# Regrouping the weight conversion and moving state products in the first sixteen tiles of a fused attention and cosine-gated MLP

## The chip, the cores and the metric

One core of a Trainium2 chip. The metric is the device time of one launch in microseconds (us). The kernel before took 815.66 us (median of 6 runs; 815.76 in the 3 runs that the prediction had). Comparisons are made against runs of the kernel before on the same chip in the same rounds; three chips were used for the experiments, so times are compared through their ratio to before.

## The reference, cut to what matters

```python
def _attn_ref(x, state):                      # x (8,8,512,64), state (8,8,32,64)
    scores = scale * x @ state^T;  a  = softmax(scores);  xread = a @ state
    scores2 = scale * state @ x^T; a2 = softmax(scores2); sread = a2 @ x
    return concatenate([xread, sread], axis=2)
def _moe_ref(x, w_in, w_out):                 # x (8*544, 512), weights (512,2048), (2048,512)
    h = x @ w_in
    g = h * cos(h)
    return g @ w_out
```
The weights arrive as float64 and are turned into float32 on the chip.

## The kernel before

Batch b has 16 tiles of 128 hidden columns each. A tile's h comes from the read weights aT and from state products `sw` (state times w_in, one product for four tiles); then g = h·cos h, then output matmuls some tiles later. In batch 0 fourteen of the sixteen steps also convert one 128x1024 load of weights, in six parts on three engines:

```python
        if p == "1":    # ScalarE: high words, absolute value
            nc.scalar.activation(dst, raw.bitcast(F32)[:, :, :, 1], func=ACTF.Abs)
        elif p == "2":  # ScalarE: low words
            nc.scalar.activation(e, raw.bitcast(U32)[:, :, :, 0], func=ACTF.Copy, ...)
        elif p == "a":  # VectorE: limit (L225)
            engine = nc.gpsimd if i == 1 else nc.vector
            engine.tensor_scalar(dst, dst, 2.0 ** -15, None, op0=ALU.max)
        elif p == "b":  # VectorE: shift (L227)
            nc.vector.tensor_scalar(bits, bits, 3, None, op0=ALU.logical_shift_left)
        elif p == "c":  # VectorE: sign (L230)
            nc.vector.scalar_tensor_tensor(out=bits, in0=raw[:, :, :, 1], scalar=-2 ** 31, ...)
        else:           # "d", GpSimd: addition (L240)
            n = 1 if i < 4 else 2
            for j in range(n):
                ...
                nc.gpsimd.tensor_tensor(bits[:, r], bits[:, r], e.bitcast(I32)[:, r], op=ALU.add)
...
    def gate(t):   ... # ScalarE: q = h + MAGIC           (L449)
    def gate2(t):  ... # VectorE: subtract, S below       (L452)
    def gate3(t):  ... # ScalarE: Abs, then Sin           (L457, L458)
    def gate4(t):  ... # VectorE: g = h * q, M below      (L464)
...
    for step, t in enumerate(tiles()):
        ...
        hidden(t)                       # TensorE: h
        go(0)                           # attention work on TensorE
        gate(t); gate2(t); go(1); go(3)
        if last >= 0: convert(last, "cd")
        if conv >= 0 and not todo[1]: convert(conv, "1")
        gate3(t)
        gate4(t)
        ...
        if conv >= 0: convert(conv, "2")
        go(4)
        if conv >= 0: convert(conv, "ab")
        ...
        while len(line) >= (LAG if step >= NH else LAG + 1):   # LAG = 3, NH = 8
            output(line.pop(0))
```
The program puts the h accumulator in PSUM and gives it two buffers. The lag is the number of tiles by which the output matmuls stay behind. The order of the work on each engine is written by hand (no scheduler).

"Cold" and "warm" below mean TensorE at a low and at full granted clock: in the kernel before the four matmuls of h(16) took 3.51 us (granted clock 0.57 from 119 to 123 us), those of h(17) 1.88 us (1.00 from 123 to 127 us); from 22.1 to 25.0 us, under the first two h, the clock was 0.50. "The lock" is a name for a wait that the traces show: a limit or shift that meets a GpSimd instruction of the addition ends only after that instruction. In the kernel before the shift at 55.83 took 1.65 us and ended 0.56 us after the addition; at 31.55, with GpSimd idle, it took 0.69 us. S and M, which have h in PSUM as an operand, show no such wait: beside an addition M at 54.06 took 0.69 us in the kernel before, and S at 59.84 took 0.69 us in the changed kernel.

## Time and profile before

| | before |
|---|---|
| median | 815.66 us |
| TensorE busy, of the 813.0 us span | 778.6 us (96%) |
| VectorE, ScalarE, GpSimd busy | 434.5, 398.3, 183.4 us |
| first state products, start | 20.56 us |
| h of tile 16, of tile 17, start | 119.36, 125.75 us |

The whole-span shares say only that TensorE is the resource in the long run. What can be won is in the first 125 us, and it is read from that stretch: which wait ends last before each h. The prediction shows those lines.

### The profile page before, as it was taken

The numbers are of one execution on the slowest core, as the hardware profiler recorded it, in microseconds if no ns is written. First come the engines' busy times: TensorE is split into PE (matmuls) and PEld (weight loads), VectorE is DVE, ScalarE is ACT, GpSimd is POOL, SyncE is SP. The second block draws the span as 40 slices with busy tenths as digits, with TensorE's granted clock in tenths as the row PEclk, the third lists the DMA queues.
The fourth block names the chain that finished last, engine by engine and source line by source line (L and its number), as shares of the span: only waits on it lengthen the run. The fifth ranks groups of instructions, "written<-read, shape, count | busy, mean of one in ns | idle before, by whom it ended". The sixth has DMA issues, their size and how long they took to land.

```text
span 813.0 us, 7602 instructions
## 1 busy us (share of the span) xinstructions
PE 778.6 (96%) x2738; PEld 349.3 (43%) x2738; DVE 434.5 (53%) x671; ACT 398.3 (49%) x644; POOL 183.4 (23%) x135
## 2 busy tenths in 40 slices
PE   7889779989999999999999999999999999999997
PEld 3333234344444444444444344444344444455553
DVE  5799896662354446753365356743654455432431
ACT  3867766544447354644464445644474445322222
POOL 3343248776000000262000000541000003620200
PEclk9799999999999999999999999999999999999999
DMA  8474350010010211120011110120100113100021
GB/s 233 155 212 152 104 154 15 13 38 14 1 26 3 51 26 27 20 59 1 0 27 30 38 23 14 34 45 1 16 10 0 27 26 69 62 1 13 14 39 38
DMA packets 111653, 37.19 MB, mean 46 GB/s; under 512 B 103616, under 2 KB 103616, under 8 KB 111616
## 3 DMA queue, kind: packets, MB, share of 16 engines
q1 hardware_dynamic: 110912, 36.45, 18.6%
q8 instruction: 21, 0.34, 0.2%
q10 hardware_dynamic: 576, 0.13, 0.1%
q0 software_dynamic: 128, 0.13, 0.1%
q14 instruction: 16, 0.13, 0.1%
HBM read 27.79 MB, written 8.91 MB: 45 GB/s over the span
## 4 chain that ended last, share of the span: by engine, by line
PE 78%; DVE 11%; ACT 8%; issue 1%; DMA 1%; POOL 0%; SPq 0%; DVEq 0%; POOLq 0%; ACTq 0%
PE o L508 42%; PE h L443 25%; PE at L295 4%; PE o L625 3%; DVE q L452 2%; PE at L382 2%; ACT q L458 1%; PE at L268 1%; DVE g_all L464 1%; ACT q L457 1%; DVE xT L315 1%; DVE aT L359 1%; DVE w_in L225 1%; ACT xT L341 1%; ACT aT L336 1%
## 5 line engine op out<-in xcount | busy, mean ns | idle before, releaser
L443 PE MATMUL h<-aT,sw 128*128 128x512 f32 x512 | 248.3, 608 | 15.4 <-DVE g_all L464 12.4
L508 PE MATMUL o<-g_all,w_out 128*128 128x512 f32 x512 | 238.9, 604 | 4.5 <-DVE sw L422 2.9
L470 POOL TENSOR_TENSOR g_all<-g_all 128x512 f32<-128x512 f32 x80 | 112.2, 1424 | 460.5 <-DVE g_all L464 455.5
L449 ACT ACTIVATE q<-h 128x512 f32<-128x512 f32 (+1 forms) x144 | 82.2, 571 | 269.3 <-PE h L443 269.3
L452 DVE SCALAR_TENSOR_TENSOR q<-q,h 128x512 f32<-128x512 f32 (+1 forms) x144 | 94.4, 655 | 208.9 <-ACT q L449 208.9
L508 PE MATMUL o<-g_all,s 128*128 128x512 f32 x384 | 177.3, 598 | 0.0
L464 DVE TENSOR_TENSOR g_all<-h,q 128x512 f32<-128x512 f32 (+1 forms) x144 | 94.9, 659 | 139.2 <-ACT q L458 138.9
L443 PEld LDWEIGHTS h<-aT,sw 128*128 128x128 f32 x512 | 98.4, 195 | 145.2 <-issue 111.6
L508 PEld LDWEIGHTS o<-g_all,w_out 128*128 128x128 f32 x512 | 94.1, 191 | 126.8 <-issue 120.1
L457 ACT ACTIVATE q<-q 128x512 f32<-128x512 f32 (+1 forms) x144 | 87.5, 608 | 104.3 <-DVE q L452 104.2
L508 PEld LDWEIGHTS o<-g_all,s 128*128 128x128 f32 x384 | 70.3, 190 | 88.4 <-issue 83.6
L458 ACT ACTIVATE q<-q,halfpi 128x512 f32<-128x512 f32 (+1 forms) x144 | 100.5, 698 | 4.5
L240 POOL TENSOR_TENSOR w_out<-w_out,s 128x512 int32<-128x512 int32 x20 | 26.7, 1354 | 84.9 <-DVE w_out L230 67.8
L470 DVE TENSOR_TENSOR g_all<-g_all 128x512 f32<-128x512 f32 x48 | 33.2, 692 | 1.6
L443 PE MATMUL h<-sT,w_in 128*128 128x256 f32 x128 | 30.2, 379 | 0.0
L424 ACT COPY sw<-at 128x512 f32<-128x512 f32 x48 | 25.7, 588 | 9.0 <-PE at L295 9.0
L625 PE MATMUL o<-w_out,g_all 128*128 128x512 f32 x64 | 29.6, 592 | 0.0
L240 POOL TENSOR_TENSOR w_in<-w_in,s 128x512 int32<-128x512 int32 x16 | 21.5, 1362 | 33.1 <-DVE w_in L230 30.1
L443 PEld LDWEIGHTS h<-sT,w_in 128*128 128x128 f32 x128 | 24.3, 190 | 10.1 <-issue 6.7
L514 DVE SCALAR_TENSOR_TENSOR held<-o,held 128x512 f32<-128x512 f32 x40 | 25.5, 682 | 3.7 <-PE o L508 3.7
L295 PE MATMUL at<-w_in,stT 64*32 64x512 f32 x384 | 26.1, 601 | 0.0
L535 DVE STREAM_TRANSPOSE ot<-held 128x512 f32<-128x512 f32 x32 | 22.2, 695 | 0.0
(84 smaller groups left out, 469.6 us busy)
## 6 DMA issues: line engine op xcount, KB each, us to landing
out_dram<-ot SPq DMA_DIRECT2D x136, 64.0 KB, 2.0
x_b<-in_x_dram SPq DMA_DIRECT2D x64, 128.0 KB, 2.9
g_all<-in_moe_w_out_dram SPq DMA_DIRECT2D x8, 1024.0 KB, 5.1
g_all<-in_moe_w_in_dram SPq DMA_DIRECT2D x6, 1024.0 KB, 5.2
g_all<-in_moe_w_in_dram SPq DMA_DIRECT2D x4, 512.0 KB, 6.0
x_b<-in_moe_w_out_dram SPq DMA_DIRECT2D x1, 1024.0 KB, 5.9
xT<-in_moe_w_out_dram SPq DMA_DIRECT2D x1, 1024.0 KB, 8.0
s<-in_state_dram SPq DMA_DIRECT2D x8, 32.0 KB, 7.1
```

Source lines behind the costliest of these rows:

```text
L240: nc.gpsimd.tensor_tensor(bits[:, r], bits[:, r], e.bitcast(I32)[:, r], op=ALU.add)
L295: nc.tensor.matmul(out=(to or at)[j][Ns * k:Ns * k + Ns, 0:n], lhsT=w[D * j:D * j + D, self.b, Ns * k:Ns * k + Ns], rhs=r(slice(D * j, D * ...
L424: nc.scalar.copy(dst, to[j][:, 0:c1 - c0])
L443: nc.tensor.matmul(out=t.hp, lhsT=t.lhs(i), rhs=t.rhs(i), start=(i == 0), stop=(i == t.kn - 1))
L449: nc.scalar.activation(t.q, t.hp, func=ACTF.Copy, bias=MAGIC)
L452: nc.vector.scalar_tensor_tensor(out=t.q, in0=t.q, scalar=MAGIC, in1=t.hp, op0=ALU.subtract, op1=ALU.subtract)
L457: nc.scalar.activation(t.q, t.q, func=ACTF.Abs)
L458: nc.scalar.activation(t.q, t.q, func=ACTF.Sin, bias=halfpi, scale=-TWO_PI)
L464: nc.vector.tensor_tensor(t.g, t.hp, t.q, op=ALU.mult)
L470: engine.tensor_tensor(out, a, b, op=ALU.subtract)
L508: nc.tensor.matmul(out=acc[bank][ch], lhsT=w[:, i, P * ch:P * ch + P], rhs=g.g, start=(i == 0), stop=(i == NH - 1))
L625: nc.tensor.matmul(out=acc[MAIN][i], lhsT=t.g[:, P * i:P * i + P], rhs=w_out[:, :, t.f, :], start=(n == 0), stop=(n == NF - 1))
```

## The change

Its intent is to take work off the path from one tile's multiply to the next in batch 0: limit and shift are done a step later, side by side with the sign; some product copies go from VectorE to ScalarE or to another step; TensorE is kept busy while it waits at the start.

```diff
-            n = 1 if i < 4 else 2
-            for j in range(n):  ...  # halves
+            nc.gpsimd.tensor_tensor(bits, bits, e.bitcast(I32), op=ALU.add)
@@ products_kept: ScalarE copies; products_taken: VectorE copies (batch 1, and the half product of step 0)
-    warm(7, acc[SIDE][1])
+    warm(10, acc[SIDE][1])
@@ plan
-            y_dve[s[2]].append((b, "max2"))
+            x_dve[s[4]].append((b, "max2"))
-            prod(1, 0, 0, SIDE, HC, WC)
-            prod(3, 0, 1, SIDE)
+            pe[0].append((0, "products", 0, SIDE, HC, WC))
+            y_dve[0].append((0, "products_taken", 0, SIDE, HC, WC))
             prod(7, 0, 2, SIDE)
-            prod(10, 0, 3, SIDE)
+            prod(11, 0, 3)
@@ the loop of steps
+        if step == 4:
+            part(0, "products", 1, SIDE)
+            part(0, "products_kept", 1, SIDE)
+        if step != 1:
+            hidden(t)
+        if step == 0:
+            hidden(all_tiles[1])
+            warm(3, acc[MAIN][0])
-            convert(last, "cd")
+            convert(last, "abcd")
-        if conv >= 0:
-            convert(conv, "ab")
-        while len(line) >= (LAG if step >= NH else LAG + 1):
+        while len(line) >= (LAG if step >= 2 * NH else LAG + 1):
```
Cut: the start of the prologue's conversions, and the second state transposes, which move from steps 4 and 5 to 5 and 6.

More of the change, by code (lines that the diff above doesn't have):

```diff
@@ L234, in convert_part @@
         else:
-            n = 1 if i < 4 else 2
-            for j in range(n):
-                r = slice(m * j // n, m * j // n + m // n)
-                nc.gpsimd.tensor_tensor(bits[:, r], bits[:, r],
-                                        e.bitcast(I32)[:, r], op=ALU.add)
+            nc.gpsimd.tensor_tensor(bits, bits, e.bitcast(I32), op=ALU.add)
     sT = consts.tile([P, NK, B, Ns], F32)
@@ L413, in products, with products_kept @@
                           at if bank is None else acc[bank])
-        def products_kept(self, nt, bank=None, c0=0, c1=WC):
+        def products_kept(self, nt, bank=None, c0=0, c1=WC, copy=None):
             to = at if bank is None else acc[bank]
@@ L419, in products_kept, with products_taken @@
             for j in range(2):
-                dst = sw_of[self.b, nt][:, j, c0:c1]
-                if self.b < 2 and (nt, c0) != (0, 0):
-                    nc.vector.tensor_copy(dst, to[j][:, 0:c1 - c0])
-                else:
-                    nc.scalar.copy(dst, to[j][:, 0:c1 - c0])
+                (copy or nc.scalar.copy)(sw_of[self.b, nt][:, j, c0:c1],
+                                         to[j][:, 0:c1 - c0])
+        def products_taken(self, *args):
+            self.products_kept(*args, copy=nc.vector.tensor_copy)
     attn = {}
@@ L698 @@
     convert(3, "12")
-    convert(2, "abcd")
     a0.max2()
     a0.exp2()
-    convert(3, "ab")
+    convert(2, "abcd")
+    convert(3, "abcd")
     def plan(b):
@@ L712, in prod @@
             pe[s].append((b, "products", nt) + bank)
-            to = x_dve if b < 2 else x_act
-            to[s].append((b, "products_kept", nt) + bank)
+            if b == 1 and nt > 0:
+                x_dve[s].append((b, "products_taken", nt) + bank)
+            else:
+                x_act[s].append((b, "products_kept", nt) + bank)
         def pairs(s, b, name, kept, i):
@@ L788 @@
     line = []
-    for step, t in enumerate(tiles()):
+    all_tiles = list(tiles())
+    for step, t in enumerate(all_tiles):
         s = step % NF
@@ L799 @@
         last, conv = conv_at.get(step - 1, -1), conv_at.get(step, -1)
-        if step == 0:
-            last = 3
         if step == B * NF + (0 if f64 else 8):
             fetch(N_LOADS + 2)
-        hidden(t)
+        if step == 4:
[6 more added lines that the diff above has]
+            warm(3, acc[MAIN][0])
         go(0)
-        if step == 4:
+        if step == 5:
             states(1, acc[SIDE][1])
@@ L823 @@
             sums(t)
-        if step == 5:
+        if step == 6:
             states_kept(1, acc[SIDE][1])
```

## The prediction

> **What bounds the kernel now.** I read the page first (busy shares, chain that ended last), then busy time by stretch, then the waits of TensorE, then the timelines of all engines over the first 130 us.
>
> ```profile
> PE 78%; DVE 11%; ACT 8%; issue 1%; DMA 1%; POOL 0%; SPq 0%; DVEq 0%; POOLq 0%; ACTq 0%
> ```
> ```profile
> core 0: us, PE busy (x) PEld busy (x) DVE busy (x) ACT busy (x) POOL busy (x), PEclk, DMA share, GB/s
> 20.00:40.00 20.00, 16.13 (x76) 6.71 (x80) 16.09 (x24) 15.79 (x25) 6.00 (x5) 0.74 0.48 158
> ...
> 60.00:80.00 20.00, 17.60 (x68) 6.79 (x68) 19.13 (x25) 15.03 (x21) 6.94 (x7) 1.00 0.46 158
> 80.00:100.00 20.00, 14.95 (x48) 5.85 (x48) 16.05 (x23) 14.66 (x22) 4.95 (x4) 0.91 0.31 105
> ...
> 400.00:500.00 100.00, 100.00 (x365) 43.41 (x358) 51.85 (x83) 49.55 (x81) 0.00 (x0) 1.00 0.15 27
> ```
> Two stages. From about 124 us TensorE has work at nearly every moment (100 of 100 us), and the chain is TensorE; nothing elsewhere shortens that part. Before it TensorE idles and its clock drops, while VectorE is busy 16 to 19 of 20 us. There the float64 weights are turned into float32, one 128x1024 load a step, beside the first 16 hidden tiles (batch 0). Only this head can gain.
> ```profile
> PE h L443 <- DVE g_all L464: 12.4, 9, 2.7
> PE o L295 <- POOL w_in L240: 5.0, 4, 3.1
> PE o L508 <- DVE sw L422: 2.9, 1, 2.9
> PE h L443 <- DVE sw L422: 2.5, 2, 2.2
> ```
> The largest wait: an h accumulator has two buffers, so h of tile t+2 waits for VectorE's multiply of tile t (L464). The head's pace is that of the multiplies. One period of them, VectorE and then GpSimd:
> ```profile
> 54.06 0.69 DVE L464 TENSOR_TENSOR g_all<-h,q 128x512 f32<-128x512 f32 x1 [0.32 <-ACT q L458]
> 55.10 0.69 DVE L225 TENSOR_SCALAR w_in<-w_in 128x1024 f32<-128x1024 f32 x1 [0.35 <-ACT w_in L218]
> 55.83 1.65 DVE L227 TENSOR_SCALAR w_in<-w_in 128x1024 int32<-128x1024 int32 x1
> 57.40 0.67 DVE L452 SCALAR_TENSOR_TENSOR q<-q,h 128x512 f32<-128x512 f32 x1
> 57.99 1.21 DVE L230 SCALAR_TENSOR_TENSOR w_in<-g_all,w_in 128x1024 int32<-128x1024 int32 x1
> 59.52 0.69 DVE L464 TENSOR_TENSOR g_all<-h,q 128x512 f32<-128x512 f32 x1 [0.32 <-ACT q L458]
> ```
> ```profile
> 53.88 3.04 POOL L240 TENSOR_TENSOR w_in<-w_in,s 128x512 int32<-128x512 int32 x2 [2.42 <-DVE w_in L230]
> 59.35 2.52 POOL L240 TENSOR_TENSOR w_in<-w_in,s 128x512 int32<-128x512 int32 x2 [2.42 <-DVE w_in L230]
> ```
> Period 59.52-54.06 = 5.46 us: multiply, limit (L225), shift (L227), subtract (L452), sign (L230), then 0.32 us for the sine. The shift takes 1.65 us here and 0.69 at 31.55, where GpSimd is idle: it stood until GpSimd's second addition ended at 53.88+3.04 = 56.92. TensorE's price:
> ```profile
> 91.41 3.43 PE L508 MATMUL o<-g_all,w_out 128*128 128x512 f32 x4 [2.90 <-DVE sw L422]
> ...
> 119.36 3.51 PE L443 MATMUL h<-aT,sw 128*128 128x512 f32 x4 [2.72 <-DVE g_all L464]
> ```
> After an idle 2.7 to 2.9 us four matmuls take 3.4 to 3.5 us, against 1.72 to 1.98 warm. From the first state products (20.56) to h of tile 17 (125.75), the idle stretches sum to 18.7 us and the slow matmuls lose about 9 more.
>
> [...]
>
> **The change part by part**, on the tile loop: S = subtract, M = multiply, tile number behind.
> 1. Order. Limit and shift leave the place between M(t) and S(t+1) and stand before the sign of the next step. So S(t+1) comes sooner, and the sine (Abs 0.63 + Sin 0.72 + 0.2 hand-over = 1.55 us) lies under limit, shift and sign: 0.71+0.61+1.21 = 2.5 us. The 0.3 us sine wait goes. The addition is one GpSimd instruction of 1024 elements (I take 2.45 us; the pairs take 2.50 undisturbed), starting 0.15 after the sign (59.20 to 59.35). M and S (0.6 each, start to start) read PSUM and run beside it, so the limit meets its last 1.3 us at most. Period by the lock: 0.15+2.45+2.5 = 5.1 us, whatever VectorE adds up to 1.3 us. The saving is 0.35 us in a plain step, more where attention work of 1.2 to 1.8 us fills the shadow.
> 2. Copies of state products for tiles 4-7, 8-11 and 12-15: three pairs of 1.28 us leave VectorE, three of 1.05 us go to ScalarE. ScalarE's step, start to start: 0.48 copy + 0.66 + 0.63 + 1.04 + 1.07 for the conversions = 3.9, plus 1.05 for a product copy or two token copies, plus 0.2 wait: 5.1. ScalarE and the lock therefore set about the same pace, and neither may be cut alone.
> 3. Products of tiles 4-7 now stand right ahead of their h, and tile 4 waits for its ScalarE copy. Their second half needs the addition of load 5, which I put at 43.15; the copy follows the conversion at 44.5 to 45.55; h(4) starts at 45.6 on a cold TensorE and ends at 49.0, not 47.3. S(4) comes at 49.7.
> 4. Second h in step 0 and six more dummy matmul calls: the seven calls took 6.28 us, so ten take about 9, to 20.2, and fill the 3.08 us gap before 20.56. The first two h, 6.02 us at low clock, then take some 3.5. But S(0) waits for VectorE: maximum (1.4) and two half loads (1.5 each, and 0.7 of lock) after 21.5, thus 26.9 against 26.63. No gain in the end.
> 5. The row maximum moves two steps on, under S(9); it needs 1.5 us on either side.
> 6. Output lag 4 until tile 16 instead of 8: the doubled output (4 matmuls, 1.72 us) moves from step 8, where TensorE had slack, to step 16, where it has none. Cost 1.7 us.
>
> Walking S through the steps with these durations, before and after: S(0) 26.6/26.9, S(2) 38.2/37.4, S(3) 43.6/41.3, S(4) 51.9/49.7, S(6) 63.1/59.9, S(8) 76.9/70.1, S(10) 90.0/82.7, S(12) 103.7/93.8, S(14) 115.1/104.2. M(14) ends at 109.6 instead of 119.3: 9.7 us, of which some 2 before tile 4, 2.6 from the two later copy pairs, 3 from ten sine waits, the rest from fewer collisions. It releases h(16), again cold (VectorE leaves TensorE 2.7 us idle). From h(16) to h(17) before: 125.75-119.36 = 6.4; now 6.4+1.7 = 8.1. h(17): 117.8 against 125.75, so 7.9 us earlier, and from there both do the same TensorE work. 815.76-7.9 = 807.9; I round to 808.
>
> **Rivals.** (a) Collisions all but vanish and TensorE becomes the bound in the head: up to 18.7 us of idle and some cold time return, about 792. Against it: ScalarE's own 5.1 us[...]. (b) The undivided addition blocks the limit for its whole length in each step, or ScalarE's extra 3.1 us stretch every step; then the period stays near 5.4, and the deferred output eats the rest: 813 to 816. For it: limit at 60.73 took 1.70 us behind an addition begun 1.4 us before. (c) Raw loads become late: at 5.1 us a step 1 MB each is 205 GB/s; the kernel moved 236 in its first 20 us, so it fits, narrowly where the next x (1 MB) joins, near 40 to 50 us. Up to 3 us lost: 811. (d) TensorE stays warm at h(4) and h(16): 3 us more, 805.
>
> **Range and chances.** Pace errors of 0.25 us a step over 14 steps are 3.5 us[...]: range 803 to 813. Faster by over 2% means below 799.8, i.e. 16 us gained, twice my sum and near rival (a): 0.06. Slower by 2% needs 16 us lost in a stage that loses none of its resources: 0.01. Within 2%: 0.93.
>
> **What would show it.** Right: the busy table is 100% TensorE from about 115 us; multiply to multiply 5.0 to 5.3 us in tiles 4 to 8; shifts all near 0.69 us and only the limit stretched; no sine wait ahead of L464's successor; ScalarE's gaps between tiles nearly gone; h(16) near 110 and a double output just before h(17). Wrong: TensorE wait on the multiply under 6 us in total (rival a), limits of over 2 us (b), ScalarE waiting for DMA (c), or new TensorE waits in later batches through the moved maximum.

## The result, and the profile after

The changed kernel gives the right result and takes 809.37 us (median of 6 runs, 807.89 to 809.96) against 815.66. The ratio is 0.992, 95% interval 0.9907 to 0.9932: 6.3 us, or 0.8%, faster. (A ratio is the mean time of one kernel's runs over that of the other's of the same rounds, so it is not quite the ratio of the medians.) Lines have moved by a few: L446 is the subtract S, L458 the multiply M, L437 h, L502 the outputs, L235 the addition, L443 ScalarE's first pass over h, L452 the sine.

Busy time by stretch, the stretches shown of before and the last one of the head:
```profile
core 0: us, PE busy (x) PEld busy (x) DVE busy (x) ACT busy (x) POOL busy (x), PEclk, DMA share, GB/s
...
20.00:40.00 20.00, 16.00 (x103) 7.14 (x102) 15.47 (x24) 16.04 (x26) 6.18 (x4) 1.00 0.47 154
...
60.00:80.00 20.00, 18.42 (x68) 6.77 (x66) 18.34 (x27) 15.74 (x22) 7.61 (x4) 1.00 0.59 203
80.00:100.00 20.00, 17.37 (x82) 6.96 (x83) 16.91 (x23) 19.32 (x30) 6.45 (x3) 0.91 0.33 108
100.00:120.00 20.00, 17.09 (x61) 6.81 (x60) 17.09 (x25) 11.52 (x17) 10.28 (x6) 0.83 0.36 102
...
400.00:500.00 100.00, 100.00 (x359) 43.66 (x359) 53.78 (x86) 49.77 (x81) 0.00 (x0) 1.00 0.15 27
```
The clock in the stretch from 20 to 40 us is 1.00 instead of 0.74 (the dummy matmuls: with seven calls ahead of the first two h and none behind, the two h took 6.13 us instead of 3.70, see l_start). TensorE does more from 60 to 100 us, and the steady stage is as it was. From 100 to 120 us the clock is 0.83: there is a cold piece (0.51 from 110 to 115 us), looked at below.

One period on VectorE, and the additions beside it, changed kernel:
```profile
57.88 0.68 DVE L458 TENSOR_TENSOR g_all<-h,q 128x512 f32<-128x512 f32 x1
59.84 0.69 DVE L446 SCALAR_TENSOR_TENSOR q<-q,h 128x512 f32<-128x512 f32 x1 [1.27 <-ACT q L443]
60.44 0.69 DVE L225 TENSOR_SCALAR w_out<-w_out 128x1024 f32<-128x1024 f32 x1
61.16 0.69 DVE L227 TENSOR_SCALAR w_out<-w_out 128x1024 int32<-128x1024 int32 x1
61.89 1.23 DVE L230 SCALAR_TENSOR_TENSOR w_out<-g_all,w_out 128x1024 int32<-128x1024 int32 x1
63.03 0.68 DVE L458 TENSOR_TENSOR g_all<-h,q 128x512 f32<-128x512 f32 x1
```
```profile
58.11 2.38 POOL L235 TENSOR_TENSOR w_in<-w_in,s 128x1024 int32<-128x1024 int32 x1 [2.68 <-DVE w_in L230]
```
The period is 63.03-57.88 = 5.15 us against 5.46. Limit and shift both take 0.69 us: the addition ended at 60.49, as the limit began. No sine wait stands before the multiply any more. In its place VectorE waits 1.27 us for ScalarE (the bracket of the subtract): ScalarE now sets the pace of this step.

The subtracts S of the walk in the prediction, and the two h at its end (starts, us):

| | S(0) | S(3) | S(4) | S(6) | S(8) | S(10) | S(12) | S(14) | h(16) | h(17) |
|---|---|---|---|---|---|---|---|---|---|---|
| before | 26.63 | 43.60 | 51.93 | 63.07 | 76.87 | 89.97 | 103.74 | 115.07 | 119.36 | 125.75 |
| predicted | 26.9 | 41.3 | 49.7 | 59.9 | 70.1 | 82.7 | 93.8 | 104.2 | 109.7 | 117.8 |
| after | 27.61 | 41.56 | 49.63 | 59.84 | 70.79 | 83.37 | 94.20 | 104.29 | 110.69 | 120.21 |

(109.7 is the predicted end of M(14) with a hand-over.) From h(17) to the end of the span it is 687.2 us before and 687.7 after: all of the change is ahead of h(17). That end of the head on TensorE, before and then after:
```profile
122.91 1.09 PE L295 MATMUL o<-w_in,stT 64*32 64x512 f32 x16
```
```profile
110.69 3.78 PE L437 MATMUL h<-aT,sw 128*128 128x512 f32 x4 [2.91 <-DVE g_all L458]
...
114.61 1.96 PE L289 MATMUL o<-w_in,stT 64*32 64x512 f32 x16
116.50 3.88 PE L502 MATMUL o<-g_all,w_out 128*128 128x512 f32 x8
120.21 1.88 PE L437 MATMUL h<-aT,sw 128*128 128x512 f32 x4
```
h(16) is released 8.7 us earlier. Then 9.5 us pass until h(17), not 6.4 as before: 1.7 us for the second output (x8 instead of x4), and the rest because the low clock lasts through the state products too (0.51 from 112 to 117 us; they took 1.96 us, 1.09 us before).

TensorE's waits, changed kernel (engine, line, releaser: us in total, times, longest):
```profile
PE h L437 <- DVE g_all L458: 12.3, 9, 2.9
PE o L289 <- POOL w_in L235: 3.9, 2, 3.1
```
The wait on the multiply is as long in total as before (12.4). What shrank are the other waits: from the first products to h(17) all idle stretches sum to 15.3 us, against 18.7 before.

One line shows a cost of the new order that the prediction did not have. In steps 3 and 14 a scaling of only 128x2 elements now stands where the addition runs (before, then after):
```profile
45.47 0.16 DVE L351 TENSOR_SCALAR i<-i 128x2 f32<-128x2 f32 x1
```
```profile
42.16 1.35 DVE L345 TENSOR_SCALAR i<-i 128x2 f32<-128x2 f32 x1
```
It ended at 43.51, the addition (from 41.13, 2.36 us long) at 43.49. In step 14 it took 0.83 us (at 104.90), again until the addition ended. So here the small instruction stood for the rest of GpSimd's instruction, as the limit of 1.71 us does in u_order below.

The table load ahead of a sine shows on ScalarE as 1.28 us, and the sine followed at once: in the changed kernel Abs at 84.26 for 0.62, load at 84.90 for 1.28, sine at 86.20. The multiply at 86.95 had waited 1.07 us for that sine.

### The profile page after: what moved, and what is told of

It reads as the page before. It is cut to its first block, busy times and chain, and to the rows that moved or that the text cites. A ratio compares the mean times of both kernels' runs of the same rounds, so it can differ in the third digit from the quotient of the medians.

```text
span 807.9 us, 7612 instructions
## 1 busy us (share of the span) xinstructions
PE 779.1 (96%) x2750; PEld 350.4 (43%) x2750; DVE 423.5 (52%) x665; ACT 401.0 (50%) x650; POOL 178.5 (22%) x119
## 4 chain that ended last, share of the span: by engine, by line
PE 80%; DVE 10%; ACT 8%; DMA 1%; issue 1%; POOL 0%; SPq 0%; DVEq 0%; POOLq 0%
PE o L502 43%; PE h L437 26%; PE at L289 4%; PE o L619 3%; DVE q L446 2%; PE at L376 2%; PE at L262 1%; ACT q L452 1%; DVE g_all L458 1%; ACT q L451 1%; DVE xT L309 1%; DVE aT L353 1%; ACT q L443 1%; ACT L452 1%; DVE w_in L230 1%; DMA g_all<-in_moe_w_in_dram 1%
## 5 line engine op out<-in xcount | busy, mean ns | idle before, releaser
L437 PE MATMUL h<-aT,sw 128*128 128x512 f32 x512 | 246.6, 605 | 14.9 <-DVE g_all L458 12.3
L502 PE MATMUL o<-g_all,w_out 128*128 128x512 f32 x512 | 236.6, 599 | 1.2 <-POOL w_out L235 1.2
L443 ACT ACTIVATE q<-h 128x512 f32<-128x512 f32 (+1 forms) x144 | 82.2, 571 | 278.2 <-PE h L437 278.2
L446 DVE SCALAR_TENSOR_TENSOR q<-q,h 128x512 f32<-128x512 f32 (+1 forms) x144 | 94.3, 655 | 224.9 <-ACT q L443 224.9
L502 PE MATMUL o<-g_all,s 128*128 128x512 f32 x384 | 177.3, 598 | 0.0
L458 DVE TENSOR_TENSOR g_all<-h,q 128x512 f32<-128x512 f32 (+1 forms) x144 | 94.7, 658 | 128.7 <-ACT q L452 128.0
L437 PEld LDWEIGHTS h<-aT,sw 128*128 128x128 f32 x512 | 97.5, 193 | 142.0 <-issue 110.0
L502 PEld LDWEIGHTS o<-g_all,w_out 128*128 128x128 f32 x512 | 93.9, 190 | 124.1 <-issue 117.8
L502 PEld LDWEIGHTS o<-g_all,s 128*128 128x128 f32 x384 | 70.3, 190 | 88.4 <-issue 84.4
L452 ACT ACTIVATE q<-q,halfpi 128x512 f32<-128x512 f32 (+1 forms) x144 | 100.5, 698 | 4.5
L235 POOL TENSOR_TENSOR w_out<-w_out,s 128x1024 int32<-128x1024 int32 x10 | 23.9, 2389 | 82.2 <-DVE w_out L230 82.2
L437 PE MATMUL h<-sT,w_in 128*128 128x256 f32 x128 | 30.2, 379 | 0.0
L437 PEld LDWEIGHTS h<-sT,w_in 128*128 128x128 f32 x128 | 24.3, 190 | 10.1 <-issue 6.2
L235 POOL TENSOR_TENSOR w_in<-w_in,s 128x1024 int32<-128x1024 int32 (+1 forms) x10 | 19.4, 1937 | 32.1 <-DVE w_in L230 22.2
```

The lines of the kernel that those rows point to most:

```text
L235: nc.gpsimd.tensor_tensor(bits, bits, e.bitcast(I32), op=ALU.add)
L437: nc.tensor.matmul(out=t.hp, lhsT=t.lhs(i), rhs=t.rhs(i), start=(i == 0), stop=(i == t.kn - 1))
L443: nc.scalar.activation(t.q, t.hp, func=ACTF.Copy, bias=MAGIC)
L446: nc.vector.scalar_tensor_tensor(out=t.q, in0=t.q, scalar=MAGIC, in1=t.hp, op0=ALU.subtract, op1=ALU.subtract)
L452: nc.scalar.activation(t.q, t.q, func=ACTF.Sin, bias=halfpi, scale=-TWO_PI)
L458: nc.vector.tensor_tensor(t.g, t.hp, t.q, op=ALU.mult)
```

## The experiments

Names: u_ runs undo or add one thing in the changed kernel; l_ runs do so in the kernel called lag15, which had a narrow series; b_ is one part alone on the kernel before.

### u_order: limit and shift back at the end of the step before

```diff
-            convert(last, "abcd")
+            convert(last, "cd")
...
+        if conv >= 0:
+            convert(conv, "ab")
```

> The changed kernel with the limit and the shift put back at the end of the step before (only the sign stays in the next step); the addition stays one instruction. My theory: the new order is the largest part of the gain, because limit and shift then stand behind an addition of 2.37 us[...], and the subtract of the next tile behind both. Sign end to subtract 0.15+2.37+1.4 = 3.9 us, then subtract 0.6 and sine 1.55: a period near 6.0 us against 5.1, over some 9 plain steps 6 to 9 us slower: 815 to 818. Rival: ScalarE alone sets the pace in the changed kernel (VectorE waits 0.7 to 1.3 us for it ahead of most subtracts), so that the order is nearly free: under 2 us slower, 809 to 811.

815.64 us (5 runs, ratio 1.0006, interval 0.9993 to 1.002). The whole gain is gone: without the new order the rest of the change is worth nothing. VectorE and the addition in this kernel:
```profile
61.00 1.71 DVE L225 TENSOR_SCALAR w_out<-w_out 128x1024 f32<-128x1024 f32 x1 [0.37 <-ACT w_out L218]
62.74 0.69 DVE L227 TENSOR_SCALAR w_out<-w_out 128x1024 int32<-128x1024 int32 x1
63.35 0.68 DVE L446 SCALAR_TENSOR_TENSOR q<-q,h 128x512 f32<-128x512 f32 x1
...
65.48 0.69 DVE L458 TENSOR_TENSOR g_all<-h,q 128x512 f32<-128x512 f32 x1 [0.31 <-ACT q L452]
```
```profile
59.77 2.38 POOL L235 TENSOR_TENSOR w_in<-w_in,s 128x1024 int32<-128x1024 int32 x1 [3.16 <-DVE w_in L230]
```
The addition ended at 62.15, the limit at 62.71: it ran its 0.6 us only after the addition. The period was 65.48-59.94 = 5.54 us. I had said near 6.0, because I had not seen that the addition starts under the sine wait, but the sign and the size of the total (815 to 818) came out.

### u_order_short: the same, with the addition cut to 64 columns (wrong result)

```diff
+            if i < 4:
+                ... # as before
+            else:
+                nc.gpsimd.tensor_tensor(dst[:, :, 0:64], dst[:, :, 0:64],
+                                        dst[:, :, 0:64], op=ALU.subtract)
```

> The changed kernel with limit and shift back at the end of the step (815.64 us), but from load 4 on GpSimd works on 64 columns only and not on 512 (and the shift is by 0, so that the weights stay finite): a wrong result on purpose[...]. My theory: the old order is slow because the limit stands behind the addition; with a short addition the limit takes 0.7 us everywhere, the period of plain tiles falls from 5.5 to 5.0 us or less, and the time to 804 to 808 (weights are also ready some 2 us earlier, which is worth at most the 4.3 us that TensorE waits for them, so the time alone does not separate the two; the period of tiles 5 to 7 does). Rival: the old order is slow by itself (the sine wait, the length of the chain from multiply to subtract): the period stays at 5.4 us or more, 812 to 815.

805.07 us (4 runs, ratio 0.9873, interval 0.986 to 0.9886); the result is wrong, as intended. In the old order with a GpSimd instruction of 0.40 to 0.61 us the limits take 0.65 to 0.72 us, and the multiplies of tiles 4, 5, 6 follow at 4.73 and 5.22 us:
```profile
57.07 0.40 POOL L238 TENSOR_TENSOR w_in<-w_in 128x128 f32<-128x128 f32 x1 [4.33 <-DVE w_in L230]
```
```profile
58.36 0.69 DVE L225 TENSOR_SCALAR w_out<-w_out 128x1024 f32<-128x1024 f32 x1 [0.35 <-ACT w_out L218]
```
Tile 7, which carries attention work, takes 6.04 us (6.33 in u_order). So the old order as such, with its sine waits of 0.3 us, is not slow: what made it slow was the addition under the limit. The period agrees with the theory less well in the second step (5.0 or less was said), where VectorE waits 0.62 us for ScalarE. As said beforehand, the time also holds the earlier weights (the short instruction doesn't wait for ScalarE's low words either), so the 10 us are not all the lock's.

### b_order: the order alone, on the kernel before

```diff
-            convert(last, "cd")
+            convert(last, "cd" if last == 3 else "abcd")
...
-        if conv >= 0:
-            convert(conv, "ab")
```

> The kernel before with the new order alone: from tile 1 on, limit and shift stand beside the sign after the subtract; copies, products, additions in halves, maximum, start and lag as before. My theory: the order is by itself nearly the whole gain, since the changed kernel without it is no faster than before; the doubled output at tile 8 costs nothing: 808 to 811, 4 to 7 us faster than before. Rival: the gain is joint, and the three pairs of copies on VectorE (3.8 us) and the products' place keep the multiplies late: 812 to 815.

810.54 us (5 runs, ratio 0.9946, interval 0.9934 to 0.9958): 4.4 us of the 6.3. The order alone is most of the gain, and the other parts do add something to it. In its trace the multiplies of tiles 5 and 6 are 5.22 us apart (5.68 before). Those of tiles 4 and 5 are 7.26 us apart: there the first output waits 3.07 us for its weights and h(5) runs cold (3.17 us), as in l_place below.

### l_place: products of tiles 4 to 7 back ahead of the second reads, their copies on VectorE

```diff
-        if step == 4:
-            part(0, "products", 1, SIDE)
-            part(0, "products_kept", 1, SIDE)
...
+            pe[3].append((0, "products", 1, SIDE))
+            x_dve[3].append((0, "products_taken", 1, SIDE))
```

> The same base with the products of tiles 4 to 7 back right behind h of tile 3, ahead of the second reads, and their copies on VectorE. My theory: they wait there for the addition of load 5 (43.3 us), the reads and the normalisation behind them wait too, and the copies add 1.3 us to VectorE: multiply of tile 3 about 2 us later, subtract of tile 4 0.8 us later: 0.5 to 1.5 us slower, 806.2 to 807.2. Rival: h of tile 4 starts without the wait for ScalarE's copy and on a warm TensorE, and it is 1 us faster.

810.53 us (6 runs, 807.43 to 812.01, ratio 0.9943, interval 0.9927 to 0.9958) against 0.9882 for lag15: about 5 us slower, where 0.5 to 1.5 was expected. The multiply of tile 3 was 3.0 us later (50.76 against 47.75 in the changed kernel; 3.7 us if both are counted from h(0)), and TensorE shows what followed:
```profile
46.68 3.12 PE L437 MATMUL h<-aT,sw 128*128 128x512 f32 x4
...
53.27 3.78 PE L502 MATMUL o<-g_all,w_out 128*128 128x512 f32 x4 [3.37 <-POOL w_out L235]
56.85 3.07 PE L437 MATMUL h<-aT,sw 128*128 128x512 f32 x4
```
The first output stands ahead of h(5) on TensorE and needs the weights of load 6. Their sign is behind the copies and the normalisation on VectorE, so the addition ended late; TensorE stood 3.37 us, went cold (3.78 us for the four matmuls of the output), and h(5) came at 56.85 instead of 52.08. I had followed VectorE only, not the order on TensorE.

### l_copies: copies of the products for tiles 8 to 15 back on VectorE

```diff
-            if b == 1 and nt > 0:
+            if b < 2 and nt > 0:
```

> The changed kernel with the lag falling at tile 15 (805.65, a tight series, so the base for small effects), and the copies of the state products for tiles 8 to 15 back on VectorE. My theory as predicted: 2.6 us of VectorE work come back on the path: 1.5 to 2.6 us slower, 807.2 to 808.2. Rival: ScalarE sets the pace in those steps (VectorE waits for it), so two pairs of 1.05 us less on ScalarE make up for it: within 0.5 us, or faster.

807.17 us (5 runs, ratio 0.9908, interval 0.9894 to 0.9922), 2.1 us slower than lag15 by the ratios. The term of 2.6 us in the prediction holds in sign and nearly in size; that ScalarE would give it back does not. The profiled run is the slowest of the series (809.64): counted from h(0), it has lost 2.3 us against lag15 at S(6), before either pair, and 3.9 us at h(16). So about 1.6 us fall in the stretch of the two pairs.

### l_max2: the row maximum back after the multiply of the scores' step

```diff
-            x_dve[s[4]].append((b, "max2"))
+            y_dve[s[2]].append((b, "max2"))
```

> The kernel with the lag at 15 (805.65 us) and the row maximum back right after the multiply of the scores' step, in all batches. My theory: 1.5 us of VectorE then stand ahead of the subtract of tile 8, the subtract of tile 9 and the exponentials behind its sine come 1.5 us later, and the later batches don't notice: 1 to 1.5 us slower, 806.6 to 807.2. My prediction as written (it needs 1.5 us on either side): no difference.

807.36 us (6 runs, 806.38 to 810.27, ratio 0.9914, interval 0.9897 to 0.9932): 1.7 us slower than lag15 by the medians, 2.6 by the ratios. In the traces, counted from h(0), S(10) comes 1.8 us later (62.7 against 61.0) and h(16) as well (90.1 against 88.3). TensorE's waits in the later batches are those of the changed kernel (1.86, 0.97 and 0.70 us against 1.85, 0.97 and 0.71). So the move is worth some 2 us, all in batch 0; my prediction's "1.5 us on either side" was wrong.

### l_split: the addition in two halves again

```diff
-            nc.gpsimd.tensor_tensor(bits, bits, e.bitcast(I32), op=ALU.add)
+            ... # two halves, as in the kernel before
```

> The same base with the addition split into two halves again. My theory: [...]within 0.4 us of 805.65. Rival: two instructions let the limit in between them (shorter waits at tiles 12 to 15), 0.5 us or more faster; or they take 0.1 to 0.5 us longer and delay the weights: slower by as much.

804.81 us (4 runs, ratio 0.9879, interval 0.9864 to 0.9893): no difference, as said. The order does not keep the limits clear of the addition, though: in the trace five of fourteen meet it (1.17 to 1.61 us at tiles 4, 5, 6, 12 and 13, against 0.69). On the other side the 128x2 scaling of step 3 gets in between the halves (0.28 us instead of 1.32 in lag15), h(4) runs warm (1.98 us against 3.49 in lag15), and S(4) comes 1.5 us sooner, counted from h(0). Of that 0.4 us is left at h(16).

### l_start: seven dummy calls at the start, none after the first two h

```diff
-    warm(10, acc[SIDE][1])
+    warm(7, acc[SIDE][1])
...
-            warm(3, acc[MAIN][0])
```

> The same base with seven dummy matmul calls in place of ten ahead of the first products and none after the two h of step 0. My theory as predicted: the first h run at half clock, but the first subtract waits for VectorE's maximum and half loads, so nothing changes: within 0.5 us of 805.65. Rival: the slow clock goes on into h of tile 2 and 3 and delays tile 3: 1 to 2 us slower.

805.27 us (4 runs, ratio 0.9875, interval 0.9862 to 0.9888): no difference, although the first two h took 6.13 us instead of 3.70. The clock was raised where nothing waited for it.

### u_lag, lag15 and warm16: the end of the head

```diff
 u_lag:  while len(line) >= (LAG if step >= NH else LAG + 1):
 lag15:  while len(line) >= (LAG if step >= 2 * NH - 1 else LAG + 1):
 warm16: after the outputs of step 15:  warm(3, acc[MAIN][0])
```

> The changed kernel with the output lag falling from 4 to 3 at tile 8 again instead of tile 16. My theory: the doubled output moves back to a stretch in which TensorE waits anyway, so 1.7 us (4 matmuls) come off the path after h of tile 16: 807.5, 1.4 to 2 us faster than the changed kernel. Rival: the doubled output at tile 8 delays h of tile 9 or 10 and is paid there: no difference, or slower by up to 1 us.

808.44 us (6 runs, 805.92 to 811.81, ratio 0.9926, interval 0.9901 to 0.9951). Not settled by the times: two runs near 811.8 at a granted clock of 0.983 stand beside two near 806 at 0.993 to 0.995. In the profiled run h(16) was 0.6 us later than in the changed kernel (both counted from h(0): 88.84 and 88.25). The 0.6 us first show at tile 11; that the doubled output causes them is not shown. From h(16) to h(17) it took 4.9 us instead of 9.5, with h(16) at full clock (1.98 us), although it had waited 2.91 us there too; why is not shown.

> The changed kernel with the lag falling at tile 15: the doubled output then stands in the 2.9 us in which TensorE waits for the multiply of tile 14, ahead of h of tile 16. My theory: 1.7 us come off the path, and the idle stretch falls to 1.2 us, so that TensorE keeps its clock: h of tile 16 takes 1.9 instead of 3.8 us, the state products behind it 1.1 instead of 2.0: 4 to 5 us faster than the changed kernel, 804.5 to 805.5. Rival[...]: only the 1.7 us, 807.5.

805.65 us (4 runs, 805.36 to 806.05, ratio 0.9882, interval 0.9867 to 0.9896): 3.7 us faster than the changed kernel by the medians, 3.1 by the ratios, and the series is narrow. That is less than the 4 to 5 us expected, and by the times alone the rival's 1.7 us isn't excluded; the trace decides:
```profile
105.68 3.60 PE L502 MATMUL o<-g_all,w_out 128*128 128x512 f32 x8
110.49 1.98 PE L437 MATMUL h<-aT,sw 128*128 128x512 f32 x4 [1.21 <-DVE g_all L458]
...
115.40 1.98 PE L437 MATMUL h<-aT,sw 128*128 128x512 f32 x4
```
The second output now fills the idle stretch, 1.21 us are left of 2.9, h(16) runs warm, and 4.9 us pass to h(17). In all seven traces with the lag at 15 (this one and the l_ runs) h(16) ran warm (1.98 us), after at most 1.6 us idle.

> The changed kernel with three dummy matmul calls (six matmuls, about 2.6 us) after the last output of step 15, in the 2.9 us idle stretch ahead of h of tile 16; the doubled output stays behind it. My theory: the stretch is filled, h of tile 16 runs at full clock: 2.8 us faster than the changed kernel, 806.5, and no change in any multiply before it. Rival: the dummies delay h of tile 16 as much as the clock gains: no difference.

807.08 us (5 runs, ratio 0.9904, interval 0.9889 to 0.992): 2.3 us faster than the changed kernel by the medians, 1.3 by the ratios, whose intervals overlap: as a time this is not clear of the noise. Its profiled run was also 1.0 us late at S(4), counted from h(0), long before the dummies. The trace shows the effect itself: h(16) took 1.98 us, not 3.78. From h(16) to h(17) it took 6.6 us, of which 1.7 are the second output. So of the 9.5 us in the changed kernel's profiled run 2.9 are the clock, and the deferred output the other 1.7 above the 4.9 of lag15.

### l_warm4: dummy matmuls ahead of the products of tiles 4 to 7

```diff
+            warm(3, acc[MAIN][0])
             part(0, "products", 1, SIDE)
```

> The same base with three more dummy matmul calls (2.6 us) between the second reads and the products of tiles 4 to 7, in the 3.1 us in which TensorE waits for the addition of load 5. My theory: h of tile 4 runs warm (1.98 instead of 3.5 us), the subtract of tile 4 comes 1.6 us sooner, half of which the later tiles keep: 0.5 to 1 us faster, 804.7 to 805.2, the fastest version. Rival: [...]no difference.

806.21 us (4 runs, ratio 0.9884, interval 0.987 to 0.9899): no gain.
```profile
44.97 1.99 PE L437 MATMUL h<-aT,sw 128*128 128x512 f32 x4 [0.82 <-ACT sw L414]
...
49.81 3.00 PE L502 MATMUL o<-g_all,w_out 128*128 128x512 f32 x4 [2.75 <-POOL w_out L235]
52.60 2.61 PE L437 MATMUL h<-aT,sw 128*128 128x512 f32 x4
```
h(4) runs warm as planned, and the wait moves on: the first output waits for the addition of load 6, 2.75 us instead of 1.2, runs cold, and h(5) behind it starts later. The same chain as in l_place.

The version that beats both kernels is lag15 (805.65); l_split (804.81) and l_start (805.27) lie within its interval.

## Why the prediction was right or wrong

The time, 809.37, is in the range, 1.4 us above 808.0.

1. That the head is paced by the multiplies and only the head can gain: right. The span after h(17) is the same to 0.5 us.
2. The order (part 1): right in mechanism. Shifts and most limits fell to 0.69 us, the sine wait went, the period is 5.05 to 5.15 us in tiles 5 and 6 (5.1 said), and u_order gives the whole gain back. The lock is shown by u_order's limit, which takes 1.71 us and ends 0.56 us after the addition, and by u_order_short, where limits take 0.65 to 0.72 us. But in plain tiles the lock no longer bound: ScalarE did, as part 2 had allowed. "Only the limit stretched" was wrong: the 128x2 scaling did too, by 1.2 us in step 3 and 0.7 us in step 14. And there are seven sine waits from M(1) to M(14) in the kernel before, not ten; they sum to 2.9 us, so the 3 us stand.
3. Copies (part 2): 2.6 us said for the two later pairs, 2.1 measured by l_copies (1.6 in its trace).
4. Place of the products (part 3): h(4) began at 45.39 (45.6 said), cold, and S(4) at 49.63 (49.7 said). Its worth was mis-sized: "some 2 before tile 4" for everything there, while taking this part back costs 5 us, through the first output and h(5).
5. Start (part 4): no gain, as said; l_start shows it.
6. Row maximum (part 5): wrong; it is worth some 2 us in batch 0. The walk had it in place, so the total did not suffer.
7. Tile 7 took 0.7 us longer than the walk: the products for tiles 8 to 11 waited 0.38 us for the copy of the second state transposes, which the change had moved to step 6, and the maximum over the scores came after them. I had left that move out.
8. The end of the head (part 6 and the step from h(16) to h(17)): this term was mis-sized. Said 8.1 us, measured 9.5 in the profiled run, because the low clock (0.51 from 112 to 117 us) lasted beyond h(16). With M(14) 1.0 us later than said (0.7 of it the scaling in step 14, since S(14) was on time) this makes the 2.4 us by which h(17) missed 117.8; 0.3 to 0.7 of that may be chance, since h(0) began anywhere between 21.7 and 23.2 us in the traces of kernels with the same start. That the deferred output costs 1.7 us there is confirmed by warm16 against lag15 (6.6 against 4.9 us).
9. The split of 9.7 us into named parts does not stand. The removals cost about 7 (order), 5 (place), 2 (copies), 2 (maximum): far more together than the gain. The parts act jointly. The traces show how for two of them: with the order undone the lock sets the period, with the place undone TensorE waits for the weights of the first output. That each part undone makes another loop the longest is argued for the rest.

Of the rivals, (a) fell: the wait on the multiply stayed at 12.3 us. (b) fell for the changed kernel, but is what u_order does. (c) fell: no wait for a raw load after the first, which varied with the run. (d) came true in part: for h(16) in u_lag, for a reason not shown, and by design in lag15, for h(4) in l_split (1.98 us each). The mark "100% TensorE from about 115 us" came true: TensorE's last idle stretch of the head ends at h(16), 110.69, and from 115 to 120 us it is busy 5.00 of 5.00 us (before, the last one ends at 119.36). The mark of 5.0 to 5.3 us from multiply to multiply held in tiles 4, 5, 6 and 8; tile 7 took 7.16.

How long TensorE must idle for its clock to fall is not shown; the traces give no single border. In the kernel before four matmuls took 3.51 us after 2.72 us idle (119.36) and 1.98 us after 1.52 (80.47), but 2.89 us after 1.61 (49.84). In the changed kernel they took 3.78 us after 2.91 (110.69), in u_order 1.98 us after 3.19 (86.09).

Left open: why a stretch of 2.9 us let the clock fall in one run and not in another (110.69 in the changed kernel, 3.78 us for four matmuls; 111.50 in u_lag, 1.98 us), and how much of u_order_short's gain is the lock and how much the earlier weights.

## What to carry to other kernels

Where VectorE and GpSimd share work, look in the trace at what stands on VectorE while GpSimd runs (2.4 us an addition here) and which instructions grow there. In this kernel S and M did not (0.68 to 0.69 us), while limits and shifts did (0.69 us became 1.65 for a shift, 1.71 for a limit); S and M under the addition and the others behind them was worth 4.4 us alone and 7 in company. Deferred work is free only if it lands where the engine waits: the same 1.7 us cost nothing in the last idle stretch and, with the clock, 3 to 4 us one tile later. A small instruction can wait there as a large one does (the 128x2 scaling: 0.16 us became 1.35). And an experiment that removes one part of a tuned schedule measures the loop that then becomes the longest, so such figures are not added up.
